# First block: reciprocal estimate and Newton steps of a unit in its own product's PSUM bank, done in the course of the next unit

## The chip, the cores and the metric

The kernel runs on one core of one Trainium2 chip. The metric is the device time of one execution in microseconds, as a median over runs. The engines that matter are TensorE (PE, matrix products; PEld is its weight load), VectorE (DVE), ScalarE (ACT), GpSimd (POOL), and SyncE (SP), whose queue issues most of the DMAs. SBUF is the working memory, PSUM the memory of eight banks into which PE writes its products; DVE and ACT read and write both.

## The reference

Three layers follow each other. A retention (attention without softmax, with a decay per head) gives `x`, 2304 rows of 512. A first dense layer of width 2048 has a rational activation between its two products. A second one, of width 1536, has a norm ahead of it and a gate in it.

```
ret = (q @ k.T / sqrt(64)) * D;  x = ret @ v           # D[i,j] = gamma**(i-j) for i >= j, else 0

h = x @ w_in                                            # [2304, 2048]
P = a0 + a1*h + a2*h**2 + a3*h**3
Q = 1 + |b0|*|h| + |b1|*h**2
g = P / (Q + 1e-6)
x = g @ w_out                                           # [2304, 512]

xn = x / sqrt(mean(x*x) + 1e-6) * rms_g
out = (silu(xn @ w_gate) * (xn @ w_val)) @ w_out2
```

Everything is float32. The products of the dense layers are made from a rounded part and a remainder of each operand, three matmuls for each product of tiles.

## The kernel before

The 2304 rows are cut into blocks of 384. The first dense layer goes block by block (n = 0 to 5), and in each block over 16 slices of the hidden width (j = 0 to 15). One pair of block and slice is a **unit** s = 16 n + j. A unit has three parts:

- the up product (`m1_up`, L308 to L310): 12 matmuls into one of the two "h" banks, which take turns (bank4_102 and bank5_103; the profile leaves buffer numbers out and says `bank`);
- the elementwise part. `m1_el_b` takes |h| into `ah` and starts Q and P: on ACT L339 to L341, on POOL L344 (`q`), on DVE L345 and L346 (`u`), and L346 is the last reader of `h`. `m1_el_y` makes on ACT an estimate `y` of 1/(Q + 1e-6), by a reciprocal square root (L357) and a square (L358). `m1_el_a` makes on DVE a Newton step of two instructions (L327, L328) and the product with P (L329). `m1_el_g` splits the result into the two parts of `g` (ACT L364, POOL L365);
- the down product (`m1_down`, L317, L318, L321) three units later (LAG = 3): 12 matmuls into the four accumulator banks.

The first block (n = 0, units 0 to 15) is unlike the others, since the rest of the retention and the preparation of the first layer's weights are dealt into its units. The retention (`att_jobs`) has scores on PE (L196) with a mask on DVE (L201), outputs on PE (L232, L238) with a scale on DVE (L245) and a DMA to `x1_d`, and a state on PE (L261) with sums on DVE (L275, L277). A weight tile (`Weights.step`) is loaded by SP's queue (L129) and taken apart by ACT (L141, L142, L156), DVE (L143, L147, L157) and POOL (L150).

For units 0 to 15 `y` lies where `ah` was, in SBUF, and the Newton step leaves its result in `q`; from unit 16 on `y` lies in bank 6 or 7, which the retention has used up to then. In the first block `m1_el_a`, `m1_el_y` and `m1_el_g` are called with s, and work on the units s - 2, s - 1 and s - 2.

The order on each engine is not the order of the calls: a scheduler reorders the recorded instructions by a timeline of its own, and each engine then works through its list strictly in order. So a change of a dependency moves instructions on all engines.

Of the kernel before, what the change touches and what calls it, by code (L numbers as in the profile page):

```python
# [7 lines left out]
F32 = mybir.dt.float32  # L8
# [3 lines left out]
ACTF = mybir.ActivationFunctionType  # L12
ALU = mybir.AluOpType
# [10 lines left out]
J1 = FF1 // 128  # L24
# [3 lines left out]
TA = 384  # L28
# [11 lines left out]
def retention_moe_kernel(  # L40
# [19 lines left out]
    act, dve, pool, pe, sp = nc.scalar, nc.vector, nc.gpsimd, nc.tensor, nc.sync  # L60

    def new_pool(name, bufs, side=None, on=ctx):
        return on.enter_context(
            tc.tile_pool(name=name, bufs=bufs, side=side, reuse_waits="tile")
        )
# [19 lines left out]
    cf = const.tile([128, 6], F32, name="cf")  # L85
# [6 lines left out]
    banks = [ps_p.tile([128, 512], F32, name=f"bank{i}") for i in range(8)]  # L92
# [174 lines left out]
    def att_add():  # L267
        if not pend:
            return
        c, ds = pend.pop()  # L270
        new = SS[(c + 1) % 2]
        for e in range(2):
            r = slice(64 * e, 64 * e + 64)
            if c == 0:
                dve.tensor_copy(out=new[r, :, e], in_=ds[r])  # L275
            else:
                dve.tensor_tensor(out=new[r, :, e], in0=new[r, :, e], in1=ds[r], op=ALU.add)  # L277
# [19 lines left out]
    g_t, el, mark = {}, {}, {}  # L297
    NS = NA * J1

    def m1_up(s, part=None):  # L300
        n, j = divmod(s, J1)
        x, w = x_t[n], wa.got["i", j]
        if part != 1:
            el[s] = bank("h")[:, 0:TA]
        h = el[s]
        for k in {0: (0, 1), 1: (2, 3)}.get(part, range(KD)):
            ks = slice(k * 128, k * 128 + 128)
            pe.matmul(out=h, lhsT=w[:, 0, ks], rhs=x[:, 0, k], start=(k == 0), stop=False)  # L308
            pe.matmul(out=h, lhsT=w[:, 0, ks], rhs=x[:, 1, k], start=False, stop=False)  # L309
            pe.matmul(out=h, lhsT=w[:, 1, ks], rhs=x[:, 0, k], start=False, stop=(k == KD - 1))  # L310

    def m1_down(s, part=None):
        n, j = divmod(s, J1)
        w, g = wa.got["o", j], g_t[s]
        for m in range(KD) if part != 1 else ():
            ms = slice(m * 128, m * 128 + 128)
            pe.matmul(out=acc[m], lhsT=w[:, 0, ms], rhs=g[:, 0], start=(j == 0), stop=False)  # L317
            pe.matmul(out=acc[m], lhsT=w[:, 1, ms], rhs=g[:, 0], start=False, stop=False)  # L318
        for m in range(KD) if part != 0 else ():
            ms = slice(m * 128, m * 128 + 128)  # L320
            pe.matmul(out=acc[m], lhsT=w[:, 0, ms], rhs=g[:, 1], start=False, stop=(j == J1 - 1))  # L321

    def m1_el_a(s):
        if s - 2 in el:
            y, q, u = el[s - 2]
            z = q if s - 2 < J1 else y
            dve.scalar_tensor_tensor(out=q, in0=q, scalar=1.0 + EPS, in1=y, op0=ALU.add, op1=ALU.mult)  # L327
            dve.scalar_tensor_tensor(out=z, in0=q, scalar=2.0, in1=y, op0=ALU.subtract, op1=ALU.mult)  # L328
            dve.scalar_tensor_tensor(  # L329
                out=u, in0=u, scalar=cf[:, 0:1], in1=z, op0=ALU.subtract, op1=ALU.mult  # L330
            )

    def m1_el_b(s):
        if s < NS:
            h = el[s]
            ah = t_p.tile([128, TA], F32, tag="ah", name="ah")
            q = tmp_p.tile([128, TA], F32, tag="q", name="q")
            u = tmp_p.tile([128, TA], F32, tag="u", name="u")
            act.activation(out=ah, in_=h, func=ACTF.Abs)  # L339
            act.activation(out=q, in_=ah, func=ACTF.Identity, scale=qb[:, 1:2], bias=qb[:, 0:1])  # L340
            mark["el"] = act.activation(  # L341
                out=u, in_=h, func=ACTF.Identity, scale=ncf[:, 3:4], bias=ncf[:, 2:3]
            )
            pool.tensor_tensor(out=q, in0=q, in1=ah, op=ALU.mult)  # L344
            dve.tensor_tensor(out=u, in0=u, in1=h, op=ALU.mult)  # L345
            dve.scalar_tensor_tensor(  # L346
                out=u, in0=u, scalar=cf[:, 1:2], in1=h, op0=ALU.subtract, op1=ALU.mult
            )
            el[s] = (ah, q, u)

    def m1_el_y(s):
        if s - 1 in el:
            y, q, u = el[s - 1]
            if s - 1 >= J1:
                y = banks[6 + (s - 1) % 2][:, 0:TA]
                el[s - 1] = (y, q, u)
            act.activation(out=y, in_=q, func=ACTF.Abs_reciprocal_sqrt, bias=cst[:, 0:1])  # L357
            act.activation(out=y, in_=y, func=ACTF.Square)  # L358

    def m1_el_g(s):  # L360
        if s - 2 in el:
            y, q, u = el.pop(s - 2)
            g = g_p.tile([128, 2, TA], F32R, tag="g", name="g")
            act.activation(out=g[:, 0], in_=u, func=ACTF.Copy)  # L364
            pool.tensor_tensor(out=g[:, 1], in0=u, in1=g[:, 0].bitcast(F32), op=ALU.subtract)  # L365
            g_t[s - 2] = g

    def m1_el(s):
        m1_el_a(s)
        m1_el_b(s)  # L370
        m1_el_y(s)
        m1_el_g(s)


    be = {}
# [120 lines left out]
    def be_plan(n, s):  # L496
        at(s + 1, lambda: be_evac(n))
        for m in range(KD):
            at(s + 2 + m, lambda m=m: be_sq(n, m))
            at(s + 9 + m, lambda m=m: be_xn(n, m))  # L500
        at(s + 7, lambda: be_sum(n))
        at(s + 8, lambda: be_newton(n))
        at(s + 13, lambda: be_out(n))
# [23 lines left out]
    for h in range(NH - 1, -1, -1):  # L527
        pool.tensor_tensor(
            out=dmk8[:, h], in0=dmk8[:, 0], in1=gi[:, h].to_broadcast([128, CH]), op=ALU.mult
# [28 lines left out]
    def wa_step():  # L558
        if wa.n2 < len(order) and (wa.n1 < NFREE or done >= njobs):
            wa.step(dve if wa.n1 % 4 else pool)  # L560
# [6 lines left out]
    def hook(j):  # L567
        nonlocal done
        want = min(njobs, -(-njobs * j // (4 * AJ)))
        while done < want:  # L570
            next(jobs)
            done += 1
        if done == njobs:
            next(jobs, None)

    for s in range(NS):
        n, j = divmod(s, J1)
        if n == 0:
            att_add()
            m1_el_a(s)  # L580
            m1_el_y(s)
            while wa.n2 < min(len(order), 2 * j):
                wa.step(dve if wa.n1 % 4 else pool)
            m1_up(s, 0)
            hook(4 * j + 1)
            m1_el_g(s)
            m1_up(s, 1)
            m1_el_b(s)
            wa_step()
            hook(4 * j + 2)  # L590
            for f in late.pop(s, []):
                f()
            if s >= LAG:
                m1_down(s - LAG, 0)
            hook(4 * j + 3)
            wa_step()
            if s >= LAG:
                m1_down(s - LAG, 1)
            hook(4 * j + 4)
            continue  # L600
        for f in late.pop(s, []):
            f()
        m1_up(s)
        m1_el(s)
        if s < J1 + LAG:
            wa_step()
        if s == J1 + 1:
            while wa.n2 < len(order):
                wa.step(dve)
            s_ctx.close()  # L610
            raw_b = new_pool("rawb", 2, "right")
            ft_b = new_pool("ftb", 2, "right")
            be_ctx = ExitStack()
            be_p = new_pool("be", 1, "right", be_ctx)
            wb = Weights(
                b_order, {"g": w_gate, "v": w_val, "o": w_out2}, alloc_b, 1, (raw_b, ft_b)
            )
            wb.load()
            wb.load()
        if n == NA - 1 and j in (6, 9, 12, 15):  # L620
            with tc.issue_after(mark["el"].ins):
                wb.step(dve)
        if s >= LAG:
            m1_down(s - LAG)
            if (s - LAG) % J1 == J1 - 1:
                be_plan((s - LAG) // J1, s)

    m1_el(NS)
    m2_up(0, 0)
    m1_down(NS - 3)  # L630
    m1_el(NS + 1)
    t_ctx.close()
    extra += [new_pool("wl", 2)] * 2
# [137 lines left out]
```

## Time and profile before

| | |
|---|---|
| median of 3 runs | 1016.67 us (1013.99 to 1016.67) |
| span of the profiled execution, first to last instruction | 1007.5 us |
| the runs' median over that span | 9.2 us (the profiled execution has no other time of its own) |
| PE busy | 973.0 us (97%) |
| DVE busy | 588.1 us (58%) |
| ACT busy | 550.5 us (55%) |
| POOL busy | 394.8 us (39%) |

Shares over the whole span mix stages with different limits. From some 210 us on PE is the engine that hardly stops; before that the retention, the weights and the first block run together. The second part of the page shows it in 40 slices of 25 us: DVE has a 9 in slices 2 to 7, and only there, and the one 8 of the granted TensorE clock (PEclk) lies there too, in slice 3. A busy PE row is modelled (matmuls overlap), so what an engine waits for is read from the waits and the timeline.

### The profile page before, as it was taken

Reading aid. Unit: us, or ns where it says so; the run is one execution under the profiler, and the core shown is the slowest. Engines: PE = TensorE matmul, PEld = TensorE weight load, DVE = VectorE, ACT = ScalarE, POOL = GpSimd, SP = SyncE. Lnnn points to the kernel's source line nnn. Section 1 sums busy time; section 2 is a strip of 40 time slices with the busy share of each in tenths; the row PEclk is TensorE's granted clock in tenths of the full one; section 3 lists DMA queues with packets and bytes.
Section 4 is the critical chain, followed back from the end, with each engine's and each line's share of the span. In section 5 each row is a group of like instructions: output and inputs, shape, how many; then the busy total and the mean of one; then the engine's idle time right before and its main releaser. Section 6 shows DMA issues by size and latency. Waiting matters only on the chain.

```text
span 1007.5 us, 14953 instructions
## 1 busy us (share of the span) xinstructions
PE 973.0 (97%) x5726; PEld 910.8 (90%) x5726; DVE 588.1 (58%) x993; ACT 550.5 (55%) x1076; POOL 394.8 (39%) x358
## 2 busy tenths in 40 slices
PE   8889899989999999999989999999999999999998
PEld 6778677889999999999989989999999999999997
DVE  5999999768667676676787676554212212212211
ACT  4867666687877877878878665554212112111111
POOL 4665676674664655746646423334001001000000
PEclk9989999999999999999999999999999999999999
DMA  9747676400100101001012343333100100000000
GB/s 315 251 144 253 203 232 200 134 25 32 32 2 32 33 1 43 21 32 32 22 52 95 102 139 125 125 117 110 49 1 17 48 1 16 32 1 1 32 1 32
DMA packets 37592, 78.91 MB, mean 78 GB/s; under 512 B 5904, under 2 KB 21392, under 8 KB 37520
## 3 DMA queue, kind: packets, MB, share of 16 engines
q1 hardware_dynamic: 36512, 77.61, 23.7%
q8 instruction: 45, 0.74, 0.3%
q10 hardware_dynamic: 1008, 0.34, 0.2%
q14 instruction: 27, 0.22, 0.1%
HBM read 64.57 MB, written 13.37 MB: 77 GB/s over the span
## 4 chain that ended last, share of the span: by engine, by line
PE 68%; DVE 6%; ACT 4%; POOL 2%; issue 2%; DMA 1%; DVEq 0%; POOLq 0%; ACTq 0%
PE bank L438 9%; PE bank L436 9%; PE bank L437 9%; PE bank L454 5%; PE bank L453 5%; PE bank L455 5%; PE bank L308 4%; PE bank L317 4%; PE bank L309 4%; PE bank L310 4%; PE bank L318 4%; PE bank L321 4%; DVE x L417 1%; DMA raw<-in_w_val_dram 1%; POOL q L344 1%
## 5 line engine op out<-in xcount | busy, mean ns | idle before, releaser
L436 PE MATMUL bank<-x,w 128*128 128x384 f32 x528 | 177.4, 336 | 1.9 <-DVE sg L442 1.9
L438 PE MATMUL bank<-x,w 128*128 128x384 f32 x528 | 177.6, 336 | 0.0
L437 PE MATMUL bank<-x,w 128*128 128x384 f32 x528 | 177.3, 336 | 0.0
L442 DVE TENSOR_TENSOR sg<-sg,bank 128x384 f32<-128x384 f32 x72 | 39.8, 553 | 214.1 <-PE bank L438 214.0
L150 POOL TENSOR_TENSOR ft<-ft,raw 128x512 int32<-128x512 int32 x68 | 98.3, 1446 | 135.4 <-DVE ft L147 83.4
L308 PE MATMUL bank<-x,w 128*128 128x384 f32 x384 | 131.7, 344 | 5.3 <-DVE u L346 4.8
L344 POOL TENSOR_TENSOR q<-q,ah 128x384 f32<-128x384 f32 x96 | 102.2, 1065 | 80.5 <-ACT q L340 74.3
L310 PE MATMUL bank<-x,w 128*128 128x384 f32 x384 | 130.8, 341 | 1.1 <-POOL w L157 0.6
L318 PE MATMUL bank<-g,w 128*128 128x384 f32 x384 | 125.9, 343 | 6.1 <-DVE w L157 6.1
L309 PE MATMUL bank<-x,w 128*128 128x384 f32 x384 | 130.0, 339 | 1.3 <-DVE x L212 1.3
L317 PE MATMUL bank<-g,w 128*128 128x384 f32 x384 | 126.2, 344 | 3.3 <-ACT g L364 3.3
L365 POOL TENSOR_TENSOR g<-u,g 128x384 fp32r<-128x384 f32 x96 | 100.5, 1048 | 70.5 <-issue 34.5
L441 ACT ACTIVATE sg<-bank 128x384 f32<-128x384 f32 x72 | 35.3, 490 | 157.0 <-PE bank L438 157.0
L212 POOL TENSOR_TENSOR x<-xr,x 128x384 fp32r<-128x384 f32 x44 | 46.1, 1061 | 158.5 <-ACT x L211 158.4
L436 PEld LDWEIGHTS bank<-x,w 128*128 128x128 f32 x528 | 99.3, 188 | 5.7 <-DVE sg L442 2.2
L437 PEld LDWEIGHTS bank<-x,w 128*128 128x128 f32 x528 | 99.3, 188 | 3.0 <-POOL x L212 0.3
L438 PEld LDWEIGHTS bank<-x,w 128*128 128x128 f32 x528 | 99.3, 188 | 0.1
L444 ACT ACTIVATE y<-sg 128x384 fp32r<-128x384 f32 x72 | 37.6, 523 | 101.3 <-DVE sg L442 100.5
L345 DVE TENSOR_TENSOR u<-u,bank 128x384 f32<-128x384 f32 x96 | 52.8, 550 | 58.1 <-ACT u L341 57.4
L321 PE MATMUL bank<-g,w 128*128 128x384 f32 x384 | 86.5, 339 | 0.0
L308 PEld LDWEIGHTS bank<-x,w 128*128 128x128 f32 x384 | 72.9, 190 | 8.3 <-DVE u L346 6.2
L318 PEld LDWEIGHTS bank<-g,w 128*128 128x128 f32 x384 | 72.4, 191 | 8.8 <-DVE w L157 7.5
(97 smaller groups left out, 2062.1 us busy)
## 6 DMA issues: line engine op xcount, KB each, us to landing
raw<-in_w_out_dram SPq DMA_DIRECT2D x28, 512.0 KB, 3.5
xb<-in_qkT_dram SPq DMA_DIRECT2D x19, 512.0 KB, 4.1
kv<-in_kv_dram SPq DMA_DIRECT2D x16, 512.0 KB, 4.6
raw<-in_w_in_dram SPq DMA_DIRECT2D x16, 512.0 KB, 4.4
raw<-in_w_gate_dram SPq DMA_DIRECT2D x12, 512.0 KB, 3.5
raw<-in_w_val_dram SPq DMA_DIRECT2D x12, 512.0 KB, 3.4
xn_d<-x SPq DMA_DIRECT2D x6, 768.0 KB, 3.8
xr<-xn_d SPq DMA_DIRECT2D x24, 192.0 KB, 2.4
```

The lines of the kernel that those rows point to most:

```text
L150: pool.tensor_tensor(out=ft, in0=ft, in1=lo, op=ALU.add)
L308: pe.matmul(out=h, lhsT=w[:, 0, ks], rhs=x[:, 0, k], start=(k == 0), stop=False)
L309: pe.matmul(out=h, lhsT=w[:, 0, ks], rhs=x[:, 1, k], start=False, stop=False)
L310: pe.matmul(out=h, lhsT=w[:, 1, ks], rhs=x[:, 0, k], start=False, stop=(k == KD - 1))
L317: pe.matmul(out=acc[m], lhsT=w[:, 0, ms], rhs=g[:, 0], start=(j == 0), stop=False)
L318: pe.matmul(out=acc[m], lhsT=w[:, 1, ms], rhs=g[:, 0], start=False, stop=False)
L321: pe.matmul(out=acc[m], lhsT=w[:, 0, ms], rhs=g[:, 1], start=False, stop=(j == J1 - 1))
L344: pool.tensor_tensor(out=q, in0=q, in1=ah, op=ALU.mult)
L365: pool.tensor_tensor(out=g[:, 1], in0=u, in1=g[:, 0].bitcast(F32), op=ALU.subtract)
L436: pe.matmul(out=t, lhsT=w[:, 0, ks], rhs=x[:, 0, k], start=(k == 0), stop=False)
L437: pe.matmul(out=t, lhsT=w[:, 0, ks], rhs=x[:, 1, k], start=False, stop=False)
L438: pe.matmul(out=t, lhsT=w[:, 1, ks], rhs=x[:, 0, k], start=False, stop=(k == KD - 1))
```

## The change

For units 0 to 14 (`early`), `y` now lies in the unit's own "h" bank, over `h`; unit 15 joins the later units in banks 6 and 7. The Newton step's second instruction writes `y` there too, and no longer `q`. So the three DVE instructions have the forms `q<-q,bank`, `bank<-q,bank` and `u<-u,cf,bank` in place of `q<-q,ah`, `q<-q,ah` and `u<-u,cf,q`. `m1_el_a` and `m1_el_g` take the unit's number, and in the first block all four parts of unit s - 1 that were left are called within unit s, with `m1_el_a` after the first half of the up product. Instructions are neither added nor taken away. Two dependencies are new: the estimate (ACT) must wait for the last reader of `h`, and the bank comes free for the up product two units later only after the product with P.

```diff
-    def m1_el_a(s):
-        if s - 2 in el:
-            y, q, u = el[s - 2]
-            z = q if s - 2 < J1 else y
+    def early(i):
+        return i < J1 - 1
+
+    def m1_el_a(i):
+        if i in el:
+            y, q, u = el[i]
             dve.scalar_tensor_tensor(out=q, in0=q, scalar=1.0 + EPS, in1=y, op0=ALU.add, op1=ALU.mult)
-            dve.scalar_tensor_tensor(out=z, in0=q, scalar=2.0, in1=y, op0=ALU.subtract, op1=ALU.mult)
+            dve.scalar_tensor_tensor(out=y, in0=q, scalar=2.0, in1=y, op0=ALU.subtract, op1=ALU.mult)
+            p = u
             dve.scalar_tensor_tensor(
-                out=u, in0=u, scalar=cf[:, 0:1], in1=z, op0=ALU.subtract, op1=ALU.mult
+                out=p, in0=u, scalar=cf[:, 0:1], in1=y, op0=ALU.subtract, op1=ALU.mult
             )
+            el[i] = p
...
-            el[s] = (ah, q, u)
+            el[s] = (h, q, u)
...
-    def m1_el_y(s):
-        if s - 1 in el:
-            y, q, u = el[s - 1]
-            if s - 1 >= J1:
-                y = banks[6 + (s - 1) % 2][:, 0:TA]
-                el[s - 1] = (y, q, u)
+    def m1_el_y(i):
+        if i in el:
+            h, q, u = el[i]
+            y = h if early(i) else banks[6 + i % 2][:, 0:TA]
+            el[i] = (y, q, u)
             act.activation(out=y, in_=q, func=ACTF.Abs_reciprocal_sqrt, bias=cst[:, 0:1])
             act.activation(out=y, in_=y, func=ACTF.Square)
...
         if n == 0:
             att_add()
-            m1_el_a(s)
-            m1_el_y(s)
+            m1_el_y(s - 1)
             while wa.n2 < min(len(order), 2 * j):
                 wa.step(dve if wa.n1 % 4 else pool)
             m1_up(s, 0)
             hook(4 * j + 1)
-            m1_el_g(s)
+            m1_el_a(s - 1)
+            m1_el_g(s - 1)
             m1_up(s, 1)
             m1_el_b(s)
```

In the changed kernel L343 to L346 are the lines that were L339 to L342, L349 and L350 the old L345 and L346, L360 and L361 the old L357 and L358, L330 and L332 the old L328 and L329, L329 the old L327, and L367 the old L364.

DVE, unit 5 of the first block (`u_882`, `q_881`, `ah_880` before), from the last reader of `h` to the product with P, in the kernel before:

```order
L346 SCALAR_TENSOR_TENSOR u_882<-u_882,cf_92,bank4_102 128x384
L327 SCALAR_TENSOR_TENSOR q_881<-q_881,ah_880 128x384
L277 TENSOR_TENSOR S0_115<-S0_115,bank7_105 64x4x64 x2
L147 SCALAR_TENSOR_TENSOR ft_658<-raw_504,ft_658 128x512
L157 TENSOR_TENSOR w_601<-ft_602,w_601 128x512
L201 TENSOR_TENSOR ret_677<-bank6_104,dmk_113 128x512
L328 SCALAR_TENSOR_TENSOR q_881<-q_881,ah_880 128x384
L245 TENSOR_TENSOR gx_114<-bank7_105,gx_114 128x512
L329 SCALAR_TENSOR_TENSOR u_882<-u_882,cf_92,q_881 128x384
```

The same stretch of the same unit (`u_888`, `q_887` now) in the changed kernel:

```order
L350 SCALAR_TENSOR_TENSOR u_888<-u_888,cf_92,bank4_102 128x384
L201 TENSOR_TENSOR ret_712<-bank6_104,dmk_113 128x512
L245 TENSOR_TENSOR gx_114<-bank7_105,gx_114 128x512
L147 SCALAR_TENSOR_TENSOR ft_783<-raw_614,ft_783 128x512
L329 SCALAR_TENSOR_TENSOR q_887<-q_887,bank4_102 128x384
L143 TENSOR_SCALAR ft_831<-ft_831 128x512
L330 SCALAR_TENSOR_TENSOR bank4_102<-q_887,bank4_102 128x384
L201 TENSOR_TENSOR ret_757<-bank6_104,dmk_113 64x4x64
L147 SCALAR_TENSOR_TENSOR ft_831<-raw_670,ft_831 128x512
L332 SCALAR_TENSOR_TENSOR u_888<-u_888,cf_92,bank4_102 128x384
```

The number of instructions between the two ends hardly moved (seven before, eight now); what moved is the place of the second operand, from SBUF (`ah`, `q`) to the bank.

ACT, the same unit, from the absolute value to the square, before:

```order
L339 ACTIVATE ah_880<-bank4_102 128x384
L341 ACTIVATE u_882<-bank4_102,ncf_93 128x384
L340 ACTIVATE q_881<-ah_880,qb_96 128x384
L142 ACTIVATE raw_561<-raw_561 128x512
L364 ACTIVATE g_871<-u_648 128x384
L141 ACTIVATE ft_658<-raw_504 128x512
L357 ACTIVATE ah_880<-q_881,cst_97 128x384
L358 ACTIVATE ah_880<-ah_880 128x384
```

And now:

```order
L343 ACTIVATE ah_886<-bank4_102 128x384
L345 ACTIVATE u_888<-bank4_102,ncf_93 128x384
L141 ACTIVATE ft_783<-raw_614 128x512
L344 ACTIVATE q_887<-ah_886,qb_96 128x384
L156 ACTIVATE w_716<-ft_717 128x512
L367 ACTIVATE g_877<-u_773 128x384
L142 ACTIVATE raw_723<-raw_723 128x512
L360 ACTIVATE bank4_102<-q_887,cst_97 128x384
L361 ACTIVATE bank4_102<-bank4_102 128x384
```

The estimate stands two instructions further from the absolute value, behind one more weight instruction (L156).

PE, where unit 1's up product (bank_102) ends and unit 2's (bank_103) begins, before:

```order
L309 MATMUL bank_102<-x,w 128x384
L310 MATMUL bank_102<-x,w 128x384
L308 MATMUL bank_103<-x,w 128x384
L309 MATMUL bank_103<-x,w 128x384
```

And now:

```order
L309 MATMUL bank_102<-x,w 128x384
L310 MATMUL bank_102<-x,w 128x384
L196 MATMUL bank_105<-xb 128x128 x4
L232 MATMUL bank_104<-xb,S_115 128x64 x4
L238 MATMUL bank_104<-ret,kv_111 64x64 x8
L196 MATMUL bank_105<-xb 128x128 x4
L196 MATMUL bank_104<-xb 128x128 x4
L238 MATMUL bank_105<-ret,kv_112 64x128 x8
L196 MATMUL bank_104<-xb 128x128 x4
L308 MATMUL bank_103<-x,w 128x384
```

Unit 2's up product has moved behind seven groups of retention matmuls, which before stood behind it.

## Rows read from the trace of the kernel before

**Rows 1.** Windows: us, busy us (instructions) by engine, granted clock, DMA share, GB/s

```profile
42.00:180.00 138.00, 125.91 (x990) 107.31 (x990) 133.73 (x197) 93.72 (x185) 89.03 (x68) 0.93 0.67 209
180.00:210.00 30.00, 25.19 (x189) 23.37 (x187) 22.06 (x35) 22.24 (x48) 22.11 (x20) 1.00 0.35 109
210.00:1007.00 797.00, 785.57 (x4260) 752.04 (x4260) 401.34 (x712) 411.57 (x801) 263.72 (x246) 1.00 0.13 44
```

**Rows 2.** Waits of DVE, 42 to 180 us: total us, times, longest

```profile
DVE gx L245 <- PE bank L238: 2.0, 2, 1.7
```

**Rows 3.** Waits of PE, 42 to 180 us

```profile
PE bank L318 <- DVE w L157: 4.4, 4, 2.0
```

**Rows 4.** DVE's instructions by form, 42 to 180 us: busy us, mean ns

```profile
L147 DVE SCALAR_TENSOR_TENSOR ft<-raw,ft 128x512 int32<-128x512 int32 x23 | 19.2, 837 | 0.1
L157 DVE TENSOR_TENSOR w<-ft,w 128x512 fp32r<-128x512 f32 x17 | 17.8, 1049 | 0.0
L143 DVE TENSOR_SCALAR ft<-ft 128x512 int32<-128x512 int32 x23 | 16.2, 706 | 0.6 <-ACT ft L141 0.5
L328 DVE SCALAR_TENSOR_TENSOR q<-q,ah 128x384 f32<-128x384 f32 x15 | 15.3, 1020 | 0.1
L329 DVE SCALAR_TENSOR_TENSOR u<-u,cf,q 128x384 f32<-128x384 f32 x15 | 14.2, 946 | 0.1
L327 DVE SCALAR_TENSOR_TENSOR q<-q,ah 128x384 f32<-128x384 f32 x15 | 13.1, 870 | 0.5 <-POOL q L344 0.3 <-ACT ah L358 0.2
```

**Rows 5.** DVE's instructions by form, 215 to 500 us

```profile
L329 DVE SCALAR_TENSOR_TENSOR u<-u,cf,bank 128x384 f32<-128x384 f32 x68 | 41.5, 610 | 1.1
L328 DVE SCALAR_TENSOR_TENSOR bank<-q,bank 128x384 f32<-128x384 f32 x67 | 37.3, 557 | 1.2
L327 DVE SCALAR_TENSOR_TENSOR q<-q,bank 128x384 f32<-128x384 f32 x66 | 36.3, 550 | 25.0 <-ACT bank L358 22.0 <-POOL q L344 1.4 <-POOL g L365 1.3
```

**Rows 6.** Line 327: duration ns min/median/max, first and last start

```profile
L327 DVE SCALAR_TENSOR_TENSOR q<-q,bank x80: 534/553/558, 206.9 to 548.5; 128x384 f32<-128x384 f32 x80
L327 DVE SCALAR_TENSOR_TENSOR q<-q,ah x16: 542/781/1637, 42.8 to 194.2; 128x384 f32<-128x384 f32 x16
```

**Rows 7.** Timeline of DVE, 104 to 142 us: start us, us

```profile
110.86 1.26 DVE L327 SCALAR_TENSOR_TENSOR q<-q,ah 128x384 f32<-128x384 f32 x1
112.16 0.56 DVE L328 SCALAR_TENSOR_TENSOR q<-q,ah 128x384 f32<-128x384 f32 x1
...
128.36 0.61 DVE L346 SCALAR_TENSOR_TENSOR u<-u,cf,bank 128x384 f32<-128x384 f32 x1
...
135.00 0.62 DVE L329 SCALAR_TENSOR_TENSOR u<-u,cf,q 128x384 f32<-128x384 f32 x1
```

**Rows 8.** Timeline of POOL, same stretch

```profile
110.42 1.29 POOL L150 TENSOR_TENSOR ft<-ft,raw 128x512 int32<-128x512 int32 x1 [0.65 <-DVE ft L147]
```

**Rows 9.** Timeline of DVE, 178 to 216 us: unit 15

```profile
194.21 1.36 DVE L327 SCALAR_TENSOR_TENSOR q<-q,ah 128x384 f32<-128x384 f32 x1
195.61 1.55 DVE L328 SCALAR_TENSOR_TENSOR q<-q,ah 128x384 f32<-128x384 f32 x1
197.19 1.24 DVE L329 SCALAR_TENSOR_TENSOR u<-u,cf,q 128x384 f32<-128x384 f32 x1
```

**Rows 10.** Timeline of PE, 175 to 216 us: its waits

```profile
199.09 0.98 PE L318 MATMUL bank<-g,w 128*128 128x384 f32 x4 [1.65 <-DVE w L157]
...
209.99 0.44 PE L317 MATMUL bank<-g,w 128*128 128x384 f32 x1 [2.76 <-ACT g L364]
```

**Rows 11.** Timeline of ACT, 104 to 142 us

```profile
129.36 0.62 ACT L357 ACTIVATE ah<-q,cst 128x384 f32<-128x384 f32 x1
```

**Rows 12.** ACT's instructions by form, 50 to 215 us: estimate in a bank

```profile
L357 ACT ACTIVATE bank<-q,cst 128x384 f32<-128x384 f32 x4 | 2.4, 608 | 0.0
```

**Rows 13.** Timeline of PE, 118 to 142 us: first matmul of two units, same bank

```profile
121.38 0.44 PE L308 MATMUL bank<-x,w 128*128 128x384 f32 x1
...
140.77 0.44 PE L308 MATMUL bank<-x,w 128*128 128x384 f32 x1
```

More of the change, by code (lines that the diff above doesn't have):

```diff
@@ L348, in m1_el_b, with m1_el_g @@
             )
-            el[s] = (ah, q, u)
-    def m1_el_y(s):
-        if s - 1 in el:
-            y, q, u = el[s - 1]
-            if s - 1 >= J1:
-                y = banks[6 + (s - 1) % 2][:, 0:TA]
-                el[s - 1] = (y, q, u)
+            el[s] = (h, q, u)
[4 more added lines that the diff above has]
+            el[i] = (y, q, u)
             act.activation(out=y, in_=q, func=ACTF.Abs_reciprocal_sqrt, bias=cst[:, 0:1])
             act.activation(out=y, in_=y, func=ACTF.Square)
-    def m1_el_g(s):
-        if s - 2 in el:
-            y, q, u = el.pop(s - 2)
+    def m1_el_g(i):
+        if i in el:
+            p = el.pop(i)
             g = g_p.tile([128, 2, TA], F32R, tag="g", name="g")
-            act.activation(out=g[:, 0], in_=u, func=ACTF.Copy)
-            pool.tensor_tensor(out=g[:, 1], in0=u, in1=g[:, 0].bitcast(F32), op=ALU.subtract)
-            g_t[s - 2] = g
+            act.activation(out=g[:, 0], in_=p, func=ACTF.Copy)
+            eng = pool
+            eng.tensor_tensor(out=g[:, 1], in0=p, in1=g[:, 0].bitcast(F32), op=ALU.subtract)
+            g_t[i] = g
     def m1_el(s):
-        m1_el_a(s)
+        m1_el_a(s - 2)
         m1_el_b(s)
-        m1_el_y(s)
-        m1_el_g(s)
+        m1_el_y(s - 1)
+        m1_el_g(s - 2)
     be = {}
@@ L579, in retention_moe_kernel @@
             att_add()
-            m1_el_a(s)
-            m1_el_y(s)
+            m1_el_y(s - 1)
             while wa.n2 < min(len(order), 2 * j):
@@ L585, in retention_moe_kernel @@
             hook(4 * j + 1)
-            m1_el_g(s)
+            m1_el_a(s - 1)
+            m1_el_g(s - 1)
             m1_up(s, 1)
```

## The prediction

> **What bounds the kernel now.** I read the windows first, to see which engine is full in which stretch; then the waits, to see who is late; then DVE's instructions by form, to see why it is full; last the timeline of single units.
>
> The windows cut the execution in three [rows 1]. From 210 us on PE is busy 785.6 of 797 us. Nothing that DVE does there can give much, and the change touches nothing there. From 42 to 180 us, where the retention, the weights and the first block share the engines, DVE is busy 133.7 of 138 us (97%), PE 125.9 (91%), ACT 93.7 (68%), POOL 89.0 (65%). DVE's longest entry of idle time there is 2.0 us in two waits [rows 2]: it waits for nobody, so this stretch is as long as DVE's work. PE is close behind. It has 12.1 us of idle time (138 - 125.9), and the largest part of it is 4.4 us for the weight remainder that DVE makes at L157 [rows 3]. [...]
>
> DVE's forms say what fills it [rows 4]. The three instructions of the Newton step and the product with P take 870, 1020 and 946 ns each, 15 times each. The same three lines, with y in a bank, take 550, 557 and 610 ns in the later blocks [rows 5]. The long ones are not long by nature. L327 with SBUF operands goes from 542 to 1637 ns, and with the bank it stays within 534 to 558 over 80 instances [rows 6]. One place shows what stretches it. At 110.86 us L327 takes 1.26 us, while POOL works on L150 until 111.71 (110.42 + 1.29) [rows 7, 8]; the rest of L327 from there to 112.12 is 0.41 us, less than its shortest time, so it ran mostly or wholly after POOL. L328, with no POOL work beside it, then takes 0.56. An instruction of DVE that reads two operands from SBUF waits out POOL's. One with an operand in a bank does not even in this stretch: L346 takes 0.61 us [rows 7], as L329 with the bank does later [rows 5].
>
> **The change part by part.** *The operand's place.* In 42 to 180 us there are 15 of each instruction. They lose 15 x (0.870 - 0.550) = 4.8, 15 x (1.020 - 0.557) = 6.9 and 15 x (0.946 - 0.610) = 5.0 us: 16.8 us of DVE's 133.7.
>
> [...]
>
> *What of it comes back.* The remaining two-operand instructions of DVE meet the same POOL instructions, 68 in this stretch [rows 1]. L147, L157 and L143, 63 in all, hold 53.2 us [rows 4]. Where L327 used to wait out a POOL instruction, the next of them may now do so. At one end nothing comes back, at the other all 16.8 us do. Of DVE's 197 instructions 45 leave the contest and 63 stay, with bank operands between them that can pass while POOL works. I take a third, 5.6 us, so that 11.2 us are saved.
>
> *What PE can use.* If DVE needs 11.2 us less, PE with its 12.1 us of idle time is the next bound. Both lists are in order, and a stretch in which both are over 95% busy is not to be expected: I take 8 us, two thirds of PE's idle time, with 0 and 16.8 as ends. [...]
>
> *The tail.* Unit 15's three instructions, from 194.21 to 198.43 us, take 4.2 us with SBUF operands [rows 9], and 1.7 by the forms of rows 5. Behind them stand PE's waits of 1.65 us for L157, which follows them on DVE, and of 2.76 for ACT's L364 [rows 10]. I take 2 of the 2.5 us, with 0 and 2.5 as ends.
>
> *The new wait on ACT.* The estimate must now wait for the last reader of h. In the unit that begins at 121.38, L346 ends at 128.97 [rows 7] and the estimate starts at 129.36 all the same [rows 11], since POOL's Q is as late. So it costs nothing there. Behind it on ACT stand the square and the weight instructions, for which DVE's L143 and L157 wait; where L346 is late, this is what pays, and 0.39 us is the cover. Into a bank the estimate takes 608 ns [rows 12], against 0.62 us here.
>
> *The new hold of the bank.* In that unit the bank is filled from 121.38, and L329 ends at 135.62 [rows 7, 13]. The next up product on the same bank begins at 140.77. The bank would be free 5.1 us earlier than it is wanted, even with the Newton step at its old, late place. If the stage shortens by 8 of 138 us, the spacing of 19.4 us becomes 18.3; the hold of 14.2 falls by the saved 1.1 to 13.1, and 5.2 are left. I count nothing; the ends are 0 and the price of the third rival. The retention matmuls that now stand ahead of unit 2's up product are the same matmuls, done earlier. No instruction and no DMA is added; SP's list keeps its kinds in slightly different order, and DMA is busy 67% of the stretch [rows 1], which 6% of speed does not fill.
>
> The sum: 8 + 2 = 10 us off the profiled span of 1007.5, which is 997.5. The runs' median lies 9.2 us above that span; with that, 1006.7 us.
>
> **The rivals.** [...]
>
> *Nothing of it.* All of the waits on POOL move to L143, L147 and L157, or the waits change hands while PE stays at its 125.9 us and its waits for weights; the tail gives 1 us: 1015.7. For it: PE's largest wait is for L157, which keeps both operands in SBUF [rows 3, 4], and the removed instructions are not what PE waits for by name. Against it: DVE has no idle time, so whatever leaves its list brings L157 forward.
>
> *PE waits for the bank.* DVE's list has, between the last reader of h and the product with P, L201 and L245 which wait for PE. If PE stands at an up product that waits for this very product with P, and matmuls that those need stand behind it, the two engines wait by turns. From 10/15 = 0.67 us of it in each of 15 units the gain is gone. At 1.2 us a unit, about what PE waits at L318 at a time (4.4 us in 4 waits, [rows 3]), it is 15 x 1.2 = 18 us against 10: 8 slower, 1024.7. For it: only two banks. Against it: the 5 us of cover above.
>
> **How the numbers follow.** The likeliest, 1006.7, with a range of its own from 1001 to 1012, has 0.56; the whole 0.20; nothing 0.15; the bank 0.09. A difference of 0.3% (3.1 us) is about what a measurement of this kernel can tell from no change. Faster by more has 0.56 + 0.20 and a little of "nothing": 0.78; within it 0.13; slower 0.09. The range leaves out most of the bank's case and the far end of the whole: 996 to 1017.
>
> **What would show it.** In the changed kernel's forms, the three instructions at 0.55 to 0.61 us in the first block; L143, L147 and L157 at about 0.09 us more than now on average if a third comes back (5.6 us over 63), at 0.27 if all does. DVE below 97% in the stage, PE above 91%, unit 16's up product some 10 us earlier. PE waits for L332 at an up product (L308) would show the bank's case; ACT waits for L350 at L360 of more than a microsecond in all would show the new wait at work. The prediction is wrong if the three instructions keep their long times, if the stage from 210 us on gets longer, or if PE's idle time stays at 12 us.

## The result, and the profile after

The changed kernel takes 1000.14 us (median of 4 runs, 999.66 to 1008.25), the kernel before 1015.65 us in the runs beside it (4 runs, 1013.99 to 1016.67): a ratio of 0.9899 [0.9868, 0.9929]. It is faster, and the forecast of 1006.7 us has the sign and, within its range, the size. The profiled spans are 998.4 and 1007.5 us, 9.1 us apart where 10 were forecast.

The windows of the changed kernel, cut where the stages now end (columns as in [rows 1]: us, then busy us and instructions of PE, PEld, DVE, ACT and POOL, granted clock, DMA share, GB/s):

```profile
42.00:170.00 128.00, 121.39 (x965) 107.53 (x965) 115.04 (x196) 91.12 (x185) 83.97 (x68) 0.94 0.70 225
170.00:200.00 30.00, 27.13 (x204) 25.37 (x203) 20.12 (x35) 21.38 (x46) 21.84 (x20) 0.94 0.36 110
200.00:998.00 798.00, 785.82 (x4260) 752.27 (x4260) 401.36 (x714) 412.22 (x803) 264.70 (x247) 1.00 0.14 43
```

DVE does in 128 us, with 196 instructions, what took it 138 us and 197 before: 115.0 busy in place of 133.7, now 90% of the stretch. PE went from 91 to 95%, and its idle time in the stretch from 12.1 to 6.6 us. From 200 us on nothing differs from [rows 1], so the whole gain is in the first block. Its marker is the last up matmul of unit 15, on the timelines of PE, before and then after:

```profile
197.10 0.34 PE L310 MATMUL bank<-x,w 128*128 128x384 f32 x1
```
```profile
189.00 0.33 PE L310 MATMUL bank<-x,w 128*128 128x384 f32 x1
...
192.06 0.96 PE L318 MATMUL bank<-g,w 128*128 128x384 f32 x4 [0.64 <-POOL w L157]
...
200.53 0.44 PE L317 MATMUL bank<-g,w 128*128 128x384 f32 x1 [2.65 <-ACT g L367]
```

8.1 us are won up to there, and 9.5 at the first down matmul of the tail (209.99 in [rows 10]). The mean granted clock up to the marker is 0.95 in both.

DVE's forms of the changed kernel, 42 to 170 us (busy us, mean ns; L329, L330 and L332 are L327, L328 and L329 of before):

```profile
L147 DVE SCALAR_TENSOR_TENSOR ft<-raw,ft 128x512 int32<-128x512 int32 x23 | 20.5, 892 | 0.3
L157 DVE TENSOR_TENSOR w<-ft,w 128x512 fp32r<-128x512 f32 x17 | 17.7, 1048 | 0.1
...
L143 DVE TENSOR_SCALAR ft<-ft 128x512 int32<-128x512 int32 x23 | 13.1, 570 | 0.0
L332 DVE SCALAR_TENSOR_TENSOR u<-u,cf,bank 128x384 f32<-128x384 f32 x15 | 9.1, 606 | 0.1
...
L330 DVE SCALAR_TENSOR_TENSOR bank<-q,bank 128x384 f32<-128x384 f32 x15 | 8.3, 552 | 0.1
L329 DVE SCALAR_TENSOR_TENSOR q<-q,bank 128x384 f32<-128x384 f32 x15 | 8.2, 548 | 2.0 <-ACT bank L361 1.9
```

The three instructions have the times of the later blocks [rows 5]. L143, L147 and L157, 63 of them as in [rows 4], hold 51.3 us, less than their 53.2 before: in sum nothing has come back on them, though L147 alone went from 19.2 to 20.5. DVE now has 13.0 us of idle time for 4.3 before, spread over several waits; the largest entry before was 2.0 us [rows 2]. DVE's waits, then PE's, in the same stretch:

```profile
DVE gx L245 <- DMA x_d<-gx: 3.4, 2, 2.3
DVE u L349 <- ACT u L345: 2.0, 3, 1.5
DVE q L329 <- ACT bank L361: 1.9, 3, 0.9
```
```profile
PE bank L196 <- DVE ret L201: 4.0, 3, 2.6
PE bank L261 <- DVE gx L245: 1.4, 2, 1.0
```

PE's wait for L157 [rows 3] is gone, and there is none at L308 for L332. Each list now waits a little for the other.

Two waits of ACT that the prediction does not count show a larger difference. From 42 to 180 us, before and then after:

```profile
ACT ft L141 <- DVE w L157: 13.6, 10, 2.7
ACT g L364 <- DVE u L329: 11.9, 8, 2.7
```
```profile
ACT g L367 <- DVE u L332: 1.7, 1, 1.7
...
ACT ft L141 <- DVE w L157: 0.2, 1, 0.2
```

A weight tile is taken apart in a buffer `ft`, of which there are two (L80). ACT can begin the next tile at L141 only when DVE has read the last but one at L157. Before, ACT stood there ten times, with the rest of its list behind it. It stood almost as long ahead of the first part of `g` (L364, now L367), for the product with P that is the last of the three shortened instructions.

### The profile page after: what moved, and what is told of

The parts are those of the page before. It is cut to its first block, busy times and chain, and to the rows that moved or that the text cites. A ratio compares the mean times of both kernels' runs of the same rounds, so it can differ in the third digit from the quotient of the medians.

```text
span 998.4 us, 14966 instructions
## 1 busy us (share of the span) xinstructions
PE 970.4 (97%) x5726; PEld 912.7 (91%) x5726; DVE 567.7 (57%) x993; ACT 548.1 (55%) x1076; POOL 390.7 (39%) x358
## 4 chain that ended last, share of the span: by engine, by line
PE 73%; DVE 11%; ACT 4%; issue 4%; DMA 4%; POOL 3%; DVEq 0%; ACTq 0%; SPq 0%; POOLq 0%
PE bank L440 9%; PE bank L442 9%; PE bank L441 9%; PE bank L308 5%; PE bank L458 5%; PE bank L459 5%; PE bank L457 5%; PE bank L310 5%; PE bank L309 5%; PE bank L317 5%; PE bank L318 5%; PE bank L321 4%; DVE w L157 1%; DMA raw<-in_w_out_dram 1%; DMA x_d<-gx 1%
## 5 line engine op out<-in xcount | busy, mean ns | idle before, releaser
L150 POOL TENSOR_TENSOR ft<-ft,raw 128x512 int32<-128x512 int32 x68 | 94.8, 1396 | 119.9 <-DVE ft L147 78.4
L308 PE MATMUL bank<-x,w 128*128 128x384 f32 x384 | 132.4, 346 | 5.1 <-DVE u L350 4.8
L369 POOL TENSOR_TENSOR g<-u,g 128x384 fp32r<-128x384 f32 x96 | 100.8, 1051 | 69.5 <-issue 34.4
L317 PE MATMUL bank<-g,w 128*128 128x384 f32 x384 | 124.7, 341 | 3.2 <-ACT g L367 3.2
L318 PE MATMUL bank<-g,w 128*128 128x384 f32 x384 | 123.5, 338 | 0.6 <-POOL w L157 0.6
L349 DVE TENSOR_TENSOR u<-u,bank 128x384 f32<-128x384 f32 x96 | 52.9, 551 | 60.3 <-ACT u L345 59.5
L321 PE MATMUL bank<-g,w 128*128 128x384 f32 x384 | 85.3, 336 | 0.0
L308 PEld LDWEIGHTS bank<-x,w 128*128 128x128 f32 x384 | 73.7, 192 | 8.3 <-DVE u L350 6.6
```

Source lines behind the costliest of these rows:

```text
L150: pool.tensor_tensor(out=ft, in0=ft, in1=lo, op=ALU.add)
L369: eng.tensor_tensor(out=g[:, 1], in0=p, in1=g[:, 0].bitcast(F32), op=ALU.subtract)
```

## Experiments

All edits are to the changed kernel unless the text says otherwise. The runs of one kernel differ by several us, and most of it goes with the mean granted clock of the execution. Over 74 runs of the kernel before (0.975 to 0.992) a straight line falls by 6.6 us per 0.01 of clock, with a correlation of -0.90. The table therefore has a column with each kernel's own line read at 0.983. That reading was chosen after the first runs. The expectations speak of medians, so both are given. The readings have standard errors of 0.2 to 1.3 us, the largest for e4 and e6, and they take the clock as something that the edit leaves alone, which e6 puts in doubt. PE's idle time is the span less PE's busy time in the profiled execution; the clock hardly enters it (28.0 and 28.1 in two executions of the changed kernel at 0.986 and 0.976).

| kernel | runs | median us | ratio to before | at clock 0.983 | PE idle us |
|---|---|---|---|---|---|
| before | 74 | | 1 | 1011.6 | 34.5 |
| changed, first runs | 4 | 1000.14 | 0.9899 [0.9868, 0.9929] | 1002.4 | 28.0 |
| a1_after_again | 6 | 1002.37 | 0.9916 [0.9888, 0.9945] | 1002.6 | 28.1 |
| e1_calls_only | 12 | 1011.14 | 0.9989 [0.9969, 1.0009] | 1009.5 | 34.0 |
| e2_bank_only | 6 | 1002.94 | 0.9910 [0.9882, 0.9938] | 1002.9 | 26.8 |
| e3_product_sbuf | 7 | 1004.47 | 0.9920 [0.9890, 0.9949] | 1002.4 | 28.0 |
| e4_less_pe | 6 | 997.72 | 0.9884 [0.9862, 0.9907] | 996.2 (just beyond its runs) | 31.7 |
| e5_less_dve | 12 | 1006.35 | 0.9959 [0.9939, 0.9978] | 1005.3 | 33.9 |
| e8_less_both | 4 | 996.03 | 0.9837 [0.9807, 0.9866] | 995.3 | 31.3 |
| b1_before_less_pe | 9 | 1008.04 | 0.9949 [0.9925, 0.9973] | 1005.7 | 37.7 |
| b2_before_less_dve | 10 | 1011.89 | 0.9999 [0.9978, 1.0020] | 1013.3 | 38.2 |
| e6_g_on_dve | 10 | 1019.07 | 1.0076 [1.0047, 1.0105] | 1012.9 (beyond its runs) | 32.5 |
| e7_w_on_dve | 12 | 1009.81 | 0.9982 [0.9956, 1.0009] | 1007.1 | 34.4 |

The last columns rest on this section of the page, here of the changed kernel (998.4 - 970.4 = 28.0):

```profile
span 998.4 us, 14966 instructions
## 1 busy us (share of the span) xinstructions
PE 970.4 (97%) x5726; PEld 912.7 (91%) x5726; DVE 567.7 (57%) x993; ACT 548.1 (55%) x1076; POOL 390.7 (39%) x358
```

### Which part of the change pays

**e1_calls_only**: the calls where the change puts them, the operands in SBUF as before (unit 15 in a bank).

```diff
+            z = q if early(i) else y
-            dve.scalar_tensor_tensor(out=y, ...)
+            dve.scalar_tensor_tensor(out=z, ...)   # and in1=z in the product
-            el[s] = (h, q, u)
+            el[s] = (ah, q, u)
```

> The calls as in the changed kernel (a unit's parts within the next unit), but y in SBUF (ah) and the Newton step's result in q, as before; unit 15 in a bank. Theory (the operand's place is what pays): L329, L330 and the product with P are back at 0.85 to 1.05 us on average in the first block, DVE is again 95% or more busy from 42 to 180 us, and the time is 1011 to 1018. Rival (the earlier calls and the order that the scheduler makes of them pay): 998 to 1005, with the long instructions.

Measured 0.9989 [0.9969, 1.0009]: no difference by the medians, 2.1 us less at the same clock. The forms of its first block, 42 to 175 us, are the long ones of [rows 4]:

```profile
L331 DVE SCALAR_TENSOR_TENSOR q<-q,ah 128x384 f32<-128x384 f32 x14 | 14.6, 1041 | 0.0
L333 DVE SCALAR_TENSOR_TENSOR u<-u,cf,q 128x384 f32<-128x384 f32 x14 | 13.5, 968 | 0.1
```

ACT still stands 11.7 us at L141 for L157, and 10.4 us for the product with P. The new places of the calls give nothing by themselves. The timelines say why: up to 215 us DVE, PE and ACT begin the same instructions in the same order as in the kernel before (272 entries on DVE). So e1 moves the calls and nothing else comes of it: the scheduler makes the old lists again.

**e2_bank_only**: the operands in the bank, the calls at their old places, so that the bank is held for longer.

```diff
-        return i < J1 - 1
+        return i < J1 - 2
...
+            m1_el_a(s - 2)
             m1_el_y(s - 1)
...
-            m1_el_a(s - 1)
-            m1_el_g(s - 1)
+            m1_el_g(s - 2)
```

> y in the unit's own bank for units 0 to 13, but the calls at their old places, two units later; units 14 and 15 in banks 6 and 7. The bank is held longer. Theory: the three instructions stay at 0.55 to 0.61 us; if the hold of the bank costs nothing, 999 to 1004; if the bank's hold is what the earlier calls were needed for, PE waits for the product with P at L308 and the time is 1006 or more. Rival (the calls pay): 1011 to 1018.

Measured 0.9910, at the same clock 0.3 to 0.5 us from the changed kernel. No wait at L308 for the bank. So the gain goes with the operand's place, and the earlier calls are not needed for it. But e2 also has the order of the changed kernel: on DVE, PE and ACT the lists agree entry by entry up to 161 us, where units 14 and 15, now in banks 6 and 7, begin to differ. The operand's place thus brings two things at once, shorter instructions and new lists on every engine, and e1 and e2 do not part them.

**e3_product_sbuf**: the Newton step in the bank, but its result in `q`, so that the product with P has two SBUF operands again.

```diff
+            z = q if early(i) else y
-            dve.scalar_tensor_tensor(out=y, ...)
+            dve.scalar_tensor_tensor(out=z, ...)   # and in1=z in the product
```

> As the changed kernel, but the Newton step leaves its result in q, so that of the three instructions the product with P alone has both operands in SBUF. Theory: that one is back at 0.9 to 1.0 us (15 x 0.35 = 5 us of DVE), the other two stay at 0.55; the time is 1001 to 1006. If waits on POOL only change hands (the prediction took a third), L143, L147 and L157 fall against the changed kernel by 0.02 to 0.05 us on average; if they do not change hands, these three stay where they are in the changed kernel (0.57, 0.89, 1.05 us).

Measured 0.9920. In its forms the product is long and the other two short (546 and 545 ns), and L147 and L143 are longer than in the changed kernel, L157 is shorter:

```profile
L147 DVE SCALAR_TENSOR_TENSOR ft<-raw,ft 128x512 int32<-128x512 int32 x24 | 23.0, 962 | 0.1
L143 DVE TENSOR_SCALAR ft<-ft 128x512 int32<-128x512 int32 x24 | 17.7, 742 | 0.6 <-ACT ft L141 0.5
...
L157 DVE TENSOR_TENSOR w<-ft,w 128x512 fp32r<-128x512 f32 x18 | 14.9, 834 | 0.3 <-ACT w L156 0.2
L333 DVE SCALAR_TENSOR_TENSOR u<-u,cf,q 128x384 f32<-128x384 f32 x15 | 13.0, 870 | 0.1
```

Over all three the mean is 842 ns (55.6 us over 66) for 814 in the changed kernel, up a little, where the expectation had "fall" or "stay". About 4 us of DVE time are back on the product (15 x 264 ns), and at the same clock the time is that of the changed kernel. The gain is not in proportion to the DVE time that is saved. The lists of e3 are a third order, unlike that of before and that of the changed kernel, so the gain does not hang on the one order that the changed kernel has.

### The price of two SBUF operands beside POOL

**p1_probe** is a kernel of its own that leaves out the whole computation (its output is zeros). It repeats the Newton instruction with SBUF operands and with one in a bank, each alone, beside POOL, and mixed one to two.

```diff
+ dve.scalar_tensor_tensor(out=d, in0=a, scalar=1.5, in1=b, ...)   # b in SBUF
+ dve.scalar_tensor_tensor(out=d, in0=a, scalar=1.5, in1=t, ...)   # t in a bank
+ pool.tensor_tensor(out=h, in0=e, in1=f, op=ALU.mult)             # beside every second one
```

> Not the computation: a probe in six stretches, whose output is zeros. 24 DVE instructions of the Newton form with both operands in SBUF alone, 24 with one in a bank alone, 24 POOL products alone, then 48 DVE instructions beside 24 POOL products: all in SBUF, all with a bank, and one of three in SBUF. Theory (DVE waits out POOL): alone 0.54 and 0.55 us; beside POOL 0.7 to 1.1 us on average in SBUF and still 0.55 with a bank. Rival (the bank form is only faster where POOL is slack): the bank form is stretched too, above 0.65 us. One of three: if waits change hands, each SBUF instruction waits longer than in the stretch where all are in SBUF (more than 1.1 us); if not, it waits the same or less.

Its forms: L58 SBUF beside POOL's L57, L63 bank beside POOL's L62, L69 and L71 the mixture, L47, L50 and POOL's L53 alone.

```profile
L58 DVE SCALAR_TENSOR_TENSOR d<-a,b 128x384 f32<-128x384 f32 x48 | 43.0, 895 | 1.6
L57 POOL TENSOR_TENSOR h<-e,f 128x384 f32<-128x384 f32 x24 | 28.6, 1190 | 2.2 <-DVE e L40 0.4
L63 DVE SCALAR_TENSOR_TENSOR d<-a,bank 128x384 f32<-128x384 f32 x48 | 26.6, 554 | 1.6
...
L62 POOL TENSOR_TENSOR h<-e,f 128x384 f32<-128x384 f32 x24 | 23.9, 996 | 2.2 <-DVE e L40 0.4
L53 POOL TENSOR_TENSOR h<-e,f 128x384 f32<-128x384 f32 x24 | 23.8, 992 | 2.2 <-DVE e L40 0.4
...
L69 DVE SCALAR_TENSOR_TENSOR d<-a,bank 128x384 f32<-128x384 f32 x32 | 17.7, 554 | 1.1
L71 DVE SCALAR_TENSOR_TENSOR d<-a,b 128x384 f32<-128x384 f32 x16 | 15.8, 985 | 0.5
L47 DVE SCALAR_TENSOR_TENSOR d<-a,b 128x384 f32<-128x384 f32 x24 | 13.4, 559 | 0.8
L50 DVE SCALAR_TENSOR_TENSOR d<-a,bank 128x384 f32<-128x384 f32 x24 | 13.3, 554 | 0.8
```

Alone the two forms cost the same, 559 and 554 ns. Beside POOL the SBUF form costs 895 ns, the bank form still 554, and POOL's own instruction takes 1190 ns beside the SBUF form, 996 beside the bank form and 992 alone. Both engines gain. In the mixture the SBUF ones left lose 426 ns each in place of 336, so 16 x 0.426 = 6.8 us in all, where a third of 48 x 0.336 = 16.1 would be 5.4. Of the 10.7 us that go, 1.4 come back: 13%. At 985 ns they wait longer than the 895 where all are in SBUF, but not the 1.1 us that was expected if waits change hands.

### What holds the stage, after the change and before it

**a1_after_again** is the changed kernel, unedited, as the base for e4 and e5.

> The changed kernel once more, so that the next two are compared with it on one chip: ratio to before 0.987 to 0.993. Its profile should again show DVE at about 90% and PE at about 95% between 42 and 170 us.

Measured 0.9916, with DVE at 91 and PE at 94% from 42 to 170 us, from 997.69 us at a clock of 0.990 to 1006.87 at 0.976. Its profiled execution has a span of 1005.1 us for 998.4 in the first one, with the same PE idle time (28.1). The windows of the first 42 us, first profile and then this one:

```profile
0.00:42.00 42.00, 36.08 (x303) 27.56 (x304) 31.21 (x52) 23.34 (x46) 20.15 (x26) 0.99 0.84 289
```
```profile
0.00:42.00 42.00, 37.24 (x274) 29.44 (x274) 27.67 (x48) 20.55 (x41) 18.66 (x25) 0.84 0.77 265
```

At 0.84 PE gets through 274 instructions, at 0.99 through 303. Where the granted clock is low differs between executions of one kernel: here it is 0.50 from 12 to 24 us, in the first profile 1.00 up to 40 us and 0.50 from 44 to 48.

**e4_less_pe** leaves out the third matmul of the first block's up products (64 matmuls).

```diff
-            pe.matmul(..., rhs=x[:, 1, k], start=False, stop=False)
-            pe.matmul(out=h, lhsT=w[:, 1, ks], rhs=x[:, 0, k], ...)
+            pe.matmul(..., rhs=x[:, 1, k], start=False, stop=(n == 0 and k == KD - 1))
+            if n > 0:
+                pe.matmul(out=h, lhsT=w[:, 1, ks], rhs=x[:, 0, k], ...)
```

> The changed kernel without the third matmul of each product (L310) in the up products of the first block: 64 matmuls of 0.173 us, 11 us of PE's time, left out there. Theory (PE is now the next bound of the stage, and DVE's further saving goes into DVE's waits): 5 to 11 us faster than the changed kernel. Rival (DVE's list still sets the pace, at 90% with its waits): 0 to 3 us faster.

4.7 us below a1 by the medians, 6.4 at the same clock (its runs had 0.976 to 0.982). Of the 11 us of PE's work that are left out, about half counts.

**e5_less_dve** leaves out the second step of P (L350, L346 in the kernel before) for units 0 to 15 (16 x 0.61 us of DVE).

```diff
-            dve.scalar_tensor_tensor(out=u, in0=u, scalar=cf[:, 1:2], in1=h, ...)
+            if s >= J1:
+                dve.scalar_tensor_tensor(out=u, in0=u, scalar=cf[:, 1:2], in1=h, ...)
```

> The changed kernel without the second step of P (L350) in the first block: 16 DVE instructions of 0.605 us, 9.7 us of DVE's time, left out there. Theory (PE is the next bound): 0 to 3 us faster than the changed kernel. Rival (DVE still sets the pace): 5 to 9 us faster.

4.0 us above a1 by the medians, 2.7 at the same clock: slower with less work, which neither expectation had. DVE's waits (42 to 180 us) and ACT's show where the time went:

```profile
DVE ft L143 <- ACT ft L141: 8.3, 6, 4.1
```
```profile
ACT ft L141 <- DVE w L157: 7.2, 6, 2.5
```

The loop of the `ft` buffers is back: L157 on DVE, then L141 on ACT, then L143 on DVE. So are ACT's wait for the product with P (7.5 us, 7 times) and, on PE, waits at L308 for the bank (1.7 us in three).

**b1_before_less_pe** and **b2_before_less_dve** are the same two edits on the kernel before, and **e8_less_both** has both on the changed one.

> The kernel before, without the third matmul of the first block's up products (11 us of PE; the output is off by that part). The prediction's first step (DVE with 97% sets the length of the stage before the change): 0 to 2 us below the kernel before at the same granted clock. Rival (PE set it too, since each list waits for the other): 5 to 7 us below, as in the changed kernel.

> The kernel before, without L346 for units 0 to 15 (16 x 0.61 = 9.8 us of DVE; the output is off by that part). The prediction's first step (DVE sets the length of the stage before the change): 6 to 9 us below the kernel before, about what the change itself gives for 18 us of DVE, with PE next. Rival (it is the place of the operand beside POOL that pays and not DVE's sum of work): 0 to 2 us below.

> The changed kernel without both of the pieces taken out singly before: the third matmul of the first block's up products (64 matmuls, 11 us of PE) and L350 for units 0 to 15 (9.7 us of DVE). Theory (after the change the two lists stand level, and each by turns waits for the other): together they give more than the sum of the two, which at a granted clock of 0.983 was -6.4 for PE's and +2.8 for DVE's, so -3.6; I expect 9 to 14 us below the changed kernel. Rival (the two effects are apart, DVE's piece costs by the order it brings whatever PE does): 3 to 5 us below it.

b1 is 4.3 us below its runs of before by the medians, 5.9 at the same clock; b2 0.5 below by the medians and 1.7 above at the same clock. Both are the rival's figures: in the kernel before, PE's work counted as much as it does now, and 9.8 us less of DVE's gave nothing ([0.9978, 1.0020], so at most some 2 us). b2's windows, and DVE's waits from 42 to 180 us:

```profile
42.00:180.00 138.00, 123.33 (x1026) 105.67 (x1025) 128.18 (x187) 95.59 (x191) 90.77 (x69) 0.98 0.67 211
```
```profile
DVE ft L143 <- ACT ft L141: 3.7, 4, 1.5
DVE gx L245 <- PE bank L238: 2.6, 5, 0.7
```

DVE's busy time falls by 5.5 us and the stretch stays: DVE waits for ACT's L141 and for PE instead. ACT still waits 10.1 us for the product with P. e8 is 7.3 us below the changed kernel at the same clock, 0.9 below e4 alone, which is within e4's error. The theory wanted 9 to 14, the rival 3 to 5, so neither holds: with PE's work out of the way the piece of DVE no longer harms, and hardly helps.

One reservation covers all of these. The scheduler makes new lists for these edits, so each mixes the work left out with another order. That order can be worth several us: e5 has the three short instructions and less work, and is slower than the changed kernel. No run put the short instructions into the old order (but for unit 15 in e1), or the long ones into the new.

### Putting the idle time to use

**e6_g_on_dve** uses DVE's freed time to take the remainder of `g` off POOL, with P's product in the bank.

```diff
-            p = u
+            p = y if early(i) else u
...
-            eng = pool
+            eng = dve if early(i) else pool
```

> The changed kernel, and for units 0 to 14 the product with P is written to the bank too, and the remainder of g is made by DVE with that one bank operand, in place of POOL (15 instructions of 1.15 us off POOL, 15 of 0.55 us onto DVE, 8.3 us). If DVE's list still set the pace it would be 5 to 8 us slower than the changed kernel; if no single engine does (DVE has 12 us of waits in the stage), from 4 us faster, since POOL's reads go and g is ready earlier, to 2 us slower. The bank is held until then: PE's waits at L308 show it if that costs.

Measured 1.0076: 16.7 us above a1 by the medians, which were not taken side by side. That is twice DVE's 8.3 us and outside both expectations. Its runs had clocks of 0.961 to 0.978, and its stage 0.83:

```profile
42.00:170.00 128.00, 116.92 (x848) 103.12 (x848) 108.55 (x186) 82.18 (x164) 61.61 (x49) 0.83 0.68 225
```

How much is the clock and how much the order stays open.

**e7_w_on_dve** gives DVE all of L157, of which POOL had a part.

```diff
-            wa.step(dve if wa.n1 % 4 else pool)
+            wa.step(dve)
```

> The changed kernel with all weight remainders (L157) on DVE and none on POOL: in the stage 6 of 1.32 us off POOL, 6 of about 0.7 to 1.05 us onto DVE (4 to 6 us). If DVE's list sets the pace 3 to 6 us slower than the changed kernel; if no single engine does, within 2 us of it, or up to 3 us faster, since PE's waits for POOL's L157 go.

Measured 0.9982, 7.4 us above a1 by the medians and 4.5 at the same clock, which the expectation had for "DVE's list sets the pace". PE's waits, 36 to 200 us, show the third rival's row, as e5 and e8 do (1.7 and 2.5 us):

```profile
PE bank L308 <- DVE u L332: 2.5, 3, 1.5
```

So DVE work that is added costs, although work that is taken away does not pay; part of that cost may be the bank's. No version that does the whole work beat the changed kernel.

## Why the prediction was right, and where not

**DVE as what bounds the stage: failed.** "So this stretch is as long as DVE's work" was read from 97% busy and no named waits. b2 removes 9.8 us of it and gains nothing; b1 removes PE work and gains 4 to 6. Busy was not the same as needed: 16.8 of the 133.7 us are what 45 instructions with SBUF operands took beyond the bank forms, so needed work was at most 117 of 138 us, 85%. The trace books such a stretch as work, as in the probe, where the SBUF form is busy 895 ns beside POOL and 559 alone. The waits that the argument missed stood on an engine at 68%: ACT's 13.6 us at L141 and 11.9 at L364. That they are what held the stage was not shown.

**The operand's place: right.** Forecast 550, 557 and 610 ns, measured 548, 552 and 606. e1 and e2 show that the gain goes with it and not with the calls. How much of it is the shorter instructions and how much the lists that come with them stays open; e3, fast with a third order, speaks for the instructions. The bank as such costs nothing here: alone the probe has 554 ns with it and 559 with SBUF.

**"I take a third" comes back: failed.** L143, L147 and L157 fell by 1.9 us in place of rising by 5.6, and e1, with the long instructions, has 52.1 us over as many; the probe has 13%. L143 has one tensor operand, not two as the prediction says, and varies all the same from 408 to 1478 ns before. So DVE's busy time fell by 18.7 us, not by 11.2.

**What PE can use: right in size.** 8 us forecast, 8.1 at the marker. But the reason given, PE as the next bound behind DVE, is only half of it: PE's work counted before too. What fell is PE's idle time over the whole execution, 34.5 to 28.0 us, and of the kernels that do the whole work on the same engines those with the Newton step in the bank have it (26.8 to 28.1, where e1 has 34.0). The two errors, more saved and less of it usable, cancelled: the size was luck in part. No run shows the two upper ends, 16.8 us in the stage and 2.5 in the tail, or "the whole" with its 0.20: 8.1 and 1.4 came, at a granted clock in the stage of 0.94 for 0.93.

**The tail: 1.4 for 2.** 9.46 at the first down matmul less 8.1. The three instructions of unit 15 take 1.8 us for 4.2 [rows 9], and PE's wait at L318 fell from 1.65, for DVE's L157, to 0.64, for POOL's. In e1, which has the order of before and unit 15 alone in a bank, the way from the last up matmul to that down matmul is 11.9 us for 12.9: with the order held, 1 us comes here from the shorter instructions or from what they shift on ACT. The other wait that the prediction put behind unit 15, 2.76 for ACT's g [rows 10], was misread. ACT and DVE before:

```profile
198.47 0.52 ACT L364 ACTIVATE g<-u 128x384 fp32r<-128x384 f32 x1 [1.71 <-DVE u L329]
...
209.38 0.56 ACT L364 ACTIVATE g<-u 128x384 fp32r<-128x384 f32 x1
```
```profile
208.40 0.61 DVE L329 SCALAR_TENSOR_TENSOR u<-u,cf,bank 128x384 f32<-128x384 f32 x1
```

Unit 15's product ends at 198.43 and its g begins at 198.47. The g that PE waits for at 209.99 begins at 209.38, behind the product of a later unit, whose operand lay in a bank before the change too. So this wait could not fall, and it is 2.65 now.

**The new wait on ACT: 1.3 for 0**, in three waits at L360 for L350, just over the mark that was set for "at work" (2.8 in a1). No wait of PE shows it by name.

**The hold of the bank: no wait, but the cover was mis-sized.** 5.2 us were forecast to be left. The last reader on DVE, and PE's next use of the same bank:

```profile
117.57 0.61 DVE L332 SCALAR_TENSOR_TENSOR u<-u,cf,bank 128x384 f32<-128x384 f32 x1
```
```profile
119.04 0.44 PE L308 MATMUL bank<-x,w 128*128 128x384 f32 x1
```

0.9 us are left here, and 4.1 and 2.4 in the next two units. e2 has the longer hold without a loss; e5, e7 and e8 are where it gives way.

**The 9.2 us between span and median: misread.** Every run lies 1.7 to 2.1 us above its own span. The rest was clock: the profiled execution of before had 0.986, and six runs of that kernel at 0.986 take 1008.5 to 1009.9 us. The changed kernel at 0.986 takes 1000.2, so about 9 us are the change. The rest of the 15.5 us between the first medians would be clock: 1015.65 us is what the line of before gives at about 0.977, but the clocks of those runs are not known. The forecast span of 997.5 us came within 0.9 us of the measured 998.4; the 6.6 us between forecast and median are the 9.2 in place of 1.8, less that 0.9.

**Still open:** why 18.7 us less of DVE in these three instructions lets PE run on, and 9.8 us less in L346 does not. The loop over two `ft` buffers is the best lead (ACT's wait at L141 for L157: 13.6 us before, 11.7 in e1, 0.2 in the changed kernel and in e2), but e3 with 4.7 us is as fast, so it is not the whole. ACT's wait for the product with P sorts the kernels better: 11.9 us before, 10.4 in e1 and 10.1 in b2, which gain little or nothing, 7.5 in e5 and 6.7 in e7, which gain some, and 1.7, 1.7 and 0.6 in the changed kernel, e2 and e3; e6, slow with 3.6, does not fit. It would tell L346 from the three instructions, since these are the last before g. But no run moved this wait alone, and the order of the lists moved with it, so it is a lead and not shown. A third buffer wasn't tried.

## What to carry to other kernels

The Newton instruction of DVE with two SBUF operands beside a busy POOL cost both engines (895 ns for 559 on DVE, 1190 for 992 on POOL, in the probe). With one operand in a bank that is free for as long, the stretch was gone (554 and 996), at no cost alone (554 for 559). Compare a form's mean with its shortest time before calling an engine full, and read the waits of the engines that are not full as well. Where an edit is to test one cause, compare the lists of the engines too: two edits here moved calls, and the lists hardly moved. Before comparing medians of two kernels look at the granted clock of each run.

## What was not expected of the hardware

The mean granted clock of one and the same kernel ran from 0.975 to 0.992 and carried 6.6 us per 0.01 with it, as much as most edits here. In the kernel before, 132 of the 140 windows of 1 us from 40 to 180 us have a granted clock of 0.50 or of 1.00. If there are only these two, 0.01 of 1010 us is 20 us at 0.50, 10 of them lost if PE were full throughout and half as fast there, by an estimate from these figures. And POOL loses to DVE as well: its product takes 1190 ns beside the SBUF form, for 996 beside the bank form.
